# A long convolution and a gated MLP on one core: when tiles are loaded and turned

## The chip, the cores and the metric

The kernel runs on one core of a Trainium2 chip. The metric is device time in microseconds (us), the median of several executions; lower is better. A core has a matrix engine (TensorE, PE in the profile, with its weight loads as PEld), a vector engine (DVE), a scalar engine (ACT), a general one (POOL), and a queue that here issues every transfer (SP). Each works through its own list of instructions in order, and they wait for each other by semaphores.

## The reference

Two blocks follow each other. The first is a long convolution, done in the reference by FFT:

```
h_filt = (maximum(pos_emb @ w1, 0) @ w2) * exp(-0.01 * pos)
u = x * v                                  # (4, 12480, 128)
y = irfft(rfft(u, 2S) * rfft(h_filt, 2S))[:, :S]
x1 = (x * y).reshape(49920, 128)
```

The second is an MLP with 2048 hidden units over the 49920 rows of the first:

```
h = x1 @ w_in                              # (49920, 2048)
out = (h * cos(h)) @ w_out                 # (49920, 128)
```

All is float32.

## The kernel before

**Two streams in one list.** The convolution of each of the four batches is cut into stages of matrix products: u (products and sums on DVE and POOL, no PE work), f1 and f2 (the forward transform and the product with the filter's spectrum), i1 and i2 (the inverse transform). Each stage is a generator of units (`units`): a unit's matmuls go to a PSUM bank called cv, and its results are read out of the bank while the next unit's matmuls run. The filter, the first batch's u, f1, f2 and i1, and the tables come first, up to about 281 us. After that the rest of the convolution is woven into the MLP by a pacer.

**Tiles and chunks.** The MLP takes its rows in 98 tiles: tile 0 has 104 rows of four tokens each, the others 128 (up to 512 tokens). A tile has 16 chunks of 128 hidden units. For chunk i (`moe_up`) PE multiplies the turned tile `at` by a slice of `w_in` into a phase bank ph (line 139); ACT (L871) and DVE (L872) reduce the phase; a chunk later ACT takes the sine (L877) and DVE multiplies (L878, `moe_act`, called by `act`), which frees ph. POOL forms sums (L886, L889, L890), and seven chunks later PE multiplies by `w_out` into acca or accb (L903). The sums of a tile are read out by `moe_evict` (L918 to L924) into `ot`.

**The pacer.** `convolve` adds one step to what is owed at each chunk and runs the generators until nothing is owed. A yield is worth, for instance, 1.0 step for a unit of f1, 3.4 for one of f2, 0.8 for one of i1; i2 of the first batch takes 3.5 steps a unit, that of the next two 3.4, of the last 1.5. A unit of i2 makes 104 rows of z, which DVE forms from the bank (L585) and SP stores to memory (`zd`, L589). `made` counts these units. A stage's rest yields 3.0, scaled in i2.

**Loading and turning.** `load(n)` has SP bring the rows of tile n into one of three `at` buffers (L846). If the rows are not made yet, it first runs the convolution until they are, without counting it as owed. The rows are turned by four PE transposes of 128x128 into a cv bank (L143, `moe_turn`), which ACT copies back over the rows (L859, `moe_turned`). In the other direction a finished tile is turned back by four transposes into a phase bank (`moe_back`, L143 too), copied by ACT (L938, `moe_rows`) and stored (L949, `moe_store`).

**The batch of transposes.** Before the change, in each odd tile n, SP is given the loads of n + 1 and n + 2 at chunk 2 (`SOON`), and at chunk 10 (`AT`) all transposes come together: `act` of chunk 9 and the convolution step of chunk 10 are issued early, then `turns(n)` puts tile n + 1 into a cv bank, tiles n - 2 and n - 1 out into two phase banks, and tile n + 2 into the same cv bank as n + 1 (into a second one once the convolution is over). The output stores follow at chunk 12.

**Banks.** Eight PSUM banks: two for acca and accb, three for ph, and for cv two while the first batch's i2 runs (a table has the third) and three afterwards. A bank is handed out again in the order in which its last reader was issued.

**Order on SP.** Loads for the convolution go ahead of their unit: `tm` (tables of i2) and `xs` one unit ahead (two in the last batch), `h` and `w` for f2 two units ahead, `xt` and `vt` for u one ahead. A load waits on SP until its buffer is free, and all that stands behind it waits too.

Of the kernel before, what the change touches and what calls it, by code (L numbers as in the profile page):

```python
# [34 lines left out]
def kernel(  # L35
# [68 lines left out]
    NFC = DFF // P  # L104
# [4 lines left out]
    NALL = 1 + math.ceil((NROWS - R) / P)  # L109
# [2 lines left out]
    ALONE = 8  # L112
    XV = 36
    LATER = 96
    SOON = 2
    AT = NFC // 2 + 2
    WCOL = 256

# [22 lines left out]
    def transpose(dst, src, ident):  # L141
        n = src.shape[0]
        nc.tensor.transpose(dst, src, ident[0:n, 0:n])  # L143
# [231 lines left out]
    def filter_turn(pool, bank, pe, ident):  # L375
        pt = bank()
        for q in range(ROWS // 2):
            transpose(pt[:, q * 2 * H:(q + 1) * 2 * H], pe[:, q, :], ident)
        peT = pool.tile([P, ROWS * H], F32, name="peT", bufs=3)
        nc.scalar.copy(out=peT[:, :], in_=pt[:, 0:ROWS * H])  # L380
        return peT
# [138 lines left out]
    soon = slice(0, CB // 8), slice(CB // 8, CB)  # L520
# [316 lines left out]
    def first_row(n):  # L837
        return min(R + (n - 1) * P, NROWS) if n else 0

    def rows_of(n):  # L840
        return first_row(n + 1) - first_row(n)

    def moe_load(pool, n):
        m, row = rows_of(n), first_row(n)
        zb = pool.tile([P, G, D], F32, name="at", bufs=3)
        nc.sync.dma_start(zb[0:m, :, :], zd[row:row + m, :, :])  # L846
        zbs[n] = zb

    def moe_turn(n, pt):
        m = rows_of(n)  # L850
        for i in range(G):
            transpose(pt[:, i * m:(i + 1) * m], zbs[n][0:m, i, :], ident)

    def moe_turned(pool, n, pt):

        m, zb = rows_of(n), zbs.pop(n)
        at = zb if n else pool.tile([P, G, D], F32, name="at", bufs=3)
        ats[n] = at[:, :, :].rearrange("p g d -> p (g d)")
        nc.scalar.copy(out=ats[n][:, 0:G * m], in_=pt[:, 0:G * m])  # L859

    def phase_bank(c):
        late = made[0] == B * NG and c % 2
        return bank() if late else ps_h.tile([P, BANK], F32, name="ph")
# [12 lines left out]
    def moe_act(ph, part, scale):  # L876
        nc.scalar.activation(part, part, AF.Sin, scale=scale)  # L877
        nc.vector.tensor_tensor(part, ph, part, op=ALU.mult)  # L878
# [14 lines left out]
    def moe_down(n, pair, second, b11, b21, b22, t):  # L893

        r = rows_of(n)
        if pair == 0:
            sums[n, second] = ps_acc.tile([P, 4, P], F32, name="acc" + "ab"[second])
        acc = sums[n, second]
        todo = ((3, 6, b22), (0, 1, t[1]), (1, 4, t[0]), (2, 3, t[3])) if second else \
            ((0, 0, b11), (2, 2, b21), (1, 5, t[2]))  # L900
        for i, (place, weight, right) in enumerate(todo):
            for h in range(2):
                nc.tensor.matmul(acc[h * CB:(h + 1) * CB, place, 0:r],  # L903
                                 w_out_sb[:, pair, weight, :], right[:, h * r:(h + 1) * r],
                                 start=(pair == 0 and i == 0), stop=(pair == NFC // 2 - 1),
                                 skip_group_check=True)

    def moe_evict(pool, n, second, ot=None):
        r = rows_of(n)
        acc = sums.pop((n, second))  # L910

        def twice(a):
            return bass.AP(tensor=a.tensor, offset=a.offset, ap=[a.ap[0], [0, 2], a.ap[1]])

        if not second:
            ot = pool.tile([P, 4, P], F32, name="ot", bufs=2)
            nc.scalar.copy(out=ot[:, 2, 0:r], in_=acc[:, 0, 0:r])
            nc.vector.tensor_tensor(ot[:, 0:2, 0:r], acc[:, 1:3, 0:r], twice(ot[:, 2, 0:r]),  # L918
                                    op=ALU.add)
            return ot  # L920
        nc.vector.tensor_tensor(ot[:, 2:4, 0:r], acc[:, 0:2, 0:r], twice(ot[:, 0, 0:r]),
                                op=ALU.add)
        nc.vector.tensor_tensor(ot[:, 0, 0:r], acc[:, 1, 0:r], ot[:, 2, 0:r], op=ALU.add)
        nc.vector.tensor_tensor(ot[:, 2:4, 0:r], acc[:, 2:4, 0:r], ot[:, 2:4, 0:r], op=ALU.add)  # L924
        return ot

    def moe_back(n, ot):
        m = rows_of(n)
        pt = ps_h.tile([P, BANK], F32, name="ph")
        places = pt[:, :].rearrange("p (h i e d) -> p h e i d", h=2, e=2, d=CB)  # L930
        for i, block in enumerate((1, 2, 3, 0)):
            transpose(places[0:m, i // 2, i % 2], ot[:, block, 0:m], ident)
        return pt

    def moe_rows(n, ot, pt):

        m = rows_of(n)
        nc.scalar.copy(out=ot[0:m, :, :].rearrange("p g d -> p (g d)"), in_=pt[0:m, :])  # L938
        return ot
# [15 lines left out]
    with tc.manual_schedule():  # L955
        with tc.tile_pool(name="psum", bufs=8, space=PSUM) as psum, \
                ExitStack() as first:
            def bank():
                return psum.tile([P, BANK], F32, name="ps")
# [142 lines left out]
        ps_c = [two_banks]  # L1102
        mpool = ctx.enter_context(tc.tile_pool(name="moe", bufs=2))

        def bank():
            return ps_c[0].tile([P, BANK], F32, name="cv")


# [15 lines left out]
        def load(n):  # L1124
            while made[0] * R < first_row(n + 1):
                next(conv)
            moe_load(mpool, n)
# [3 lines left out]
        pt = bank()  # L1131
        moe_turn(0, pt)
        moe_turned(mpool, 0, pt)
        steps = [(n, c) for n in range(NALL) for c in range(NFC)]
        hidden, pairs, gates, ots, obs = {}, {}, {}, {}, {}

        def convolve():
            nonlocal owed
            owed += 1.0
            while owed > 0.0:  # L1140
                owed -= next(conv, owed)

        def act(i):
            if i in hidden:
                moe_act(*hidden.pop(i))

        def turns(n):

            ins = [k for k in (n + 1, n + 2) if k < NALL]
            outs = [(k, ots.pop(k)) for k in (n - 2, n - 1) if k in ots]  # L1150
            alone = made[0] == B * NG
            banks = [bank() for k in ins[0:1]]
            for k in ins[0:1]:
                moe_turn(k, banks[0])
                moe_turned(mpool, k, banks[0])
            copies = []
            for k, ot in outs:
                copies.append((k, ot, moe_back(k, ot)))
            for k in ins[1:2]:
                if alone:  # L1160
                    banks.append(bank())
                moe_turn(k, banks[-1])
            yield
            for k, ot, pt in copies:
                obs[k] = moe_rows(k, ot, pt)
                yield
            for k in ins[1:2]:
                moe_turned(mpool, k, banks[-1])

        for i in range(len(steps) + LAG):  # L1170
            if i >= LAG:
                pn, pc = steps[i - LAG]
                moe_down(pn, pc // 2, pc % 2, *gates[i - LAG - pc % 2])
                if pc >= NFC - 2:
                    ots[pn] = moe_evict(mpool, pn, pc % 2, ots.get(pn))
            rest = iter(())
            if i < len(steps):
                n, c = steps[i]
                both = n % 2 == 1 and c == AT
                if n == 0 and c == NFC // 2:  # L1180
                    load(1)
                if n % 2 == 1 and c == SOON:
                    for k in range(n + 1, min(n + 3, NALL)):
                        load(k)
                if n == 0 and c == NFC - 2:
                    pt = bank()
                    moe_turn(1, pt)
                    moe_turned(mpool, 1, pt)
                if both:
                    act(i - 1)  # L1190
                    convolve()
                    rest = turns(n)
                    next(rest)
                ph = phase_bank(c)
                next(rest, None)
                if c % 2 == 0:
                    pairs[i] = mpool.tile([P, 2, BANK], F32, name="gt", bufs=4)
                hidden[i] = moe_up(mpool, n, c, pairs[i - c % 2], ph)
            for _ in rest:
                pass  # L1200
            act(i - 1)
            if i - 4 in pairs:
                gates[i - 4] = moe_sums(mpool, steps[i - 4][0], pairs.pop(i - 4))
            if i < len(steps) and c == AT + 2:
                for k in sorted(obs):
                    moe_store(k, obs.pop(k))
            if i >= len(steps) or not both:
                convolve()
        for n in sorted(ots):
            moe_store(n, moe_rows(n, ots[n], moe_back(n, ots[n])))  # L1210
# [28 lines left out]
```

## Time and profile before

| | us |
|---|---|
| median of 3 runs (3618.9 to 3620.81) | 3619.49 |
| the profiled execution | 3619.85 |
| its span, first to last instruction | 3618.1 |

Stages of that execution, from windows cut at the first matmul of a chunk:

| window, us | what runs | length | PE busy | DVE | ACT | POOL |
|---|---|---|---|---|---|---|
| 0 to 281.4 | filter, first batch's forward transform, tables | 281.4 | 266.7 | 227.1 | 199.7 | 206.0 |
| 281.4 to 530.9 | tiles 0 to 6, first batch's i2, second batch's u | 249.5 | 238.6 | 208.0 | 163.8 | 216.5 |
| 530.9 to 1082.8 | tiles 7 to 22, second batch's f1, f2, i1 | 551.9 | 546.6 | 428.7 | 337.1 | 423.9 |
| 1082.8 to 1122.1 | chunk 1 of tile 23: a run of convolution alone | 39.3 | 36.5 | 30.3 | 14.0 | 3.2 |
| 1122.1 to 1961.2 | tiles 23 to 46 | 839.1 | 831.4 | 652.5 | 493.2 | 652.2 |
| 1961.2 to 1979.6 | the same kind of run in tile 47 | 18.4 | 15.5 | 11.7 | 5.0 | 3.5 |
| 1979.6 to 2816.0 | tiles 47 to 70 | 836.4 | 831.1 | 651.9 | 493.5 | 652.2 |
| 2816.0 to 2830.8 | the same kind of run in tile 71 | 14.8 | 13.6 | 11.4 | 5.1 | 3.5 |
| 2830.8 to 2960.5 | tiles 71 to 73, last batch's i2 | 129.7 | 129.7 | 79.7 | 55.8 | 60.2 |
| 2960.5 to 3618.1 | tiles 74 to 97, MLP alone | 657.6 | 650.2 | 519.8 | 452.3 | 525.9 |

A view of waits names who waited, on which tile and line, for whom, with the total, the count and the longest. The timeline merges equal instructions: start, length, engine, line, operation, tiles, shape, count, and in brackets the idle time before it with what ended it. Matmuls are pipelined, so a busy PE can still be slowed; the granted clock (1.00 is full) is a column of the windows.

### The profile page before, as it was taken

The numbers are of one execution on the slowest core, as the hardware profiler recorded it, in microseconds if no ns is written. First come the engines' busy times: TensorE is split into PE (matmuls) and PEld (weight loads), VectorE is DVE, ScalarE is ACT, GpSimd is POOL, SyncE is SP. The second block draws the span as 40 slices with busy tenths as digits, with TensorE's granted clock in tenths as the row PEclk, the third lists the DMA queues.
The fourth block names the chain that finished last, engine by engine and source line by source line (L and its number), as shares of the span: only waits on it lengthen the run. The fifth ranks groups of instructions, "written<-read, shape, count | busy, mean of one in ns | idle before, by whom it ended". The sixth has DMA issues, their size and how long they took to land.

```text
span 3618.1 us, 102337 instructions
## 1 busy us (share of the span) xinstructions
PE 3559.8 (98%) x40830; PEld 2553.9 (71%) x40830; DVE 2821.0 (78%) x5289; ACT 2219.4 (61%) x4482; POOL 2747.0 (76%) x3240
## 2 busy tenths in 40 slices
PE   9999999999999999999999999999999999999999
PEld 7996767666677777666677776766667876666666
DVE  7887886688887775688887776678887667877877
ACT  7776666656654556656554556666655446666676
POOL 7777995688864996688864887579884457878887
PEclk9999999999999999999999999999999999999999
DMA  7545540122214640022211662022220440000000
GB/s 192 157 147 158 154 125 14 37 66 71 76 32 115 172 139 27 24 72 75 66 36 48 171 175 62 13 61 66 73 71 20 133 123 25 16 22 25 16 22 17
DMA packets 224196, 281.86 MB, mean 78 GB/s; under 512 B 23386, under 2 KB 161122, under 8 KB 223594
## 3 DMA queue, kind: packets, MB, share of 16 engines
q1 hardware_dynamic: 223722, 275.30, 26.5%
q8 instruction: 326, 5.34, 0.6%
q14 instruction: 148, 1.21, 0.1%
HBM read 194.75 MB, written 80.46 MB: 76 GB/s over the span
## 4 chain that ended last, share of the span: by engine, by line
PE 86%; DVE 3%; ACT 1%; POOL 1%; DMA 1%; issue 1%; SPq 0%; ACTq 0%; DVEq 0%; POOLq 0%
PE ph L139 31%; PE accb L903 18%; PE cv L139 17%; PE acca L903 13%; PE cv L457 3%; PE cv L143 1%; PE ph L143 1%; DVE gt L872 1%; DVE gt L878 1%; ACT gt L871 0%; DMA tm<-td 0%; DVE xt L439 0%; POOL ts L886 0%; DVE t L516 0%; POOL slots L449 0%
## 5 line engine op out<-in xcount | busy, mean ns | idle before, releaser
L871 ACT ACTIVATE gt<-ph 128x512 int32<-128x512 f32 (+1 forms) x1374 | 818.9, 596 | 1165.3 <-PE ph L139 1083.5
L872 DVE SCALAR_TENSOR_TENSOR gt<-ph,gt 128x512 f32<-128x512 f32 (+1 forms) x1374 | 943.4, 687 | 681.5 <-ACT gt L871 676.7
L139 PE MATMUL ph<-at,w_in_sb 128*64 128x512 f32 (+1 forms) x5496 | 1428.5, 594 | 6.1 <-DVE gt L878 4.7
L886 POOL TENSOR_TENSOR ts<-gt 128x512 f32<-128x512 f32 (+2 forms) x784 | 1000.9, 1277 | 537.0 <-PE accb L903 525.4
L877 ACT ACTIVATE gt<-gt 128x512 f32<-128x512 f32 (+1 forms) x1568 | 973.3, 621 | 14.8 <-DVE gt L872 13.6
L878 DVE TENSOR_TENSOR gt<-ph,gt 128x512 f32<-128x512 f32 (+1 forms) x1374 | 930.9, 678 | 1.4
L903 PE MATMUL accb<-ts,w_out_sb 128*64 128x128 f32 (+2 forms) x9408 | 652.9, 272 | 0.0
L889 POOL TENSOR_TENSOR ts<-ts,gt 128x256 f32<-128x256 f32 (+2 forms) x784 | 574.0, 732 | 61.5
L890 POOL TENSOR_TENSOR ts<-gt,ts 128x256 f32<-128x256 f32 (+2 forms) x784 | 573.4, 731 | 61.5
L903 PEld LDWEIGHTS acca<-gt,w_out_sb 128*64 128x64 f32 x6272 | 403.1, 136 | 245.6 <-issue 209.5
L903 PEld LDWEIGHTS accb<-ts,w_out_sb 128*64 128x64 f32 x9408 | 546.7, 137 | 0.0
L903 PE MATMUL acca<-gt,w_out_sb 128*64 128x128 f32 (+2 forms) x6272 | 482.1, 272 | 0.0
L903 PEld LDWEIGHTS accb<-gt,w_out_sb 128*64 128x64 f32 x3136 | 228.4, 136 | 246.0 <-issue 186.4
L139 PEld LDWEIGHTS ph<-at,w_in_sb 128*64 128x64 f32 x5496 | 353.2, 137 | 28.4 <-issue 13.1
L139 PEld LDWEIGHTS cv<-slots,tm 96*40 96x40 f32 (+1 forms) x3840 | 228.6, 126 | 127.8 <-issue 118.4
L903 PE MATMUL accb<-gt,w_out_sb 128*64 128x128 f32 (+1 forms) x3136 | 314.0, 273 | 2.4 <-DVE ot L924 0.4
L903 PE MATMUL acca<-ts,w_out_sb 128*64 128x128 f32 (+1 forms) x3136 | 311.6, 272 | 2.3 <-POOL ts L889 2.3
L139 PE MATMUL cv<-slots,tm 96*40 96x128 f32 (+1 forms) x3840 | 256.0, 275 | 9.9 <-DMA tm<-td 5.5
L517 POOL TENSOR_TENSOR slots<-slots,t 120x256 f32<-120x256 f32 x288 | 210.9, 734 | 67.8 <-DVE t L516 60.8
L139 PEld LDWEIGHTS cv<-even,slots 120*33 120x33 f32 (+1 forms) x3072 | 166.7, 125 | 65.0 <-issue 58.8
L903 PEld LDWEIGHTS acca<-ts,w_out_sb 128*64 128x64 f32 x3136 | 204.5, 137 | 3.7 <-POOL ts L889 3.6
L139 PE MATMUL cv<-at,w_in_sb 128*64 128x512 f32 (+1 forms) x776 | 200.5, 587 | 0.0
(142 smaller groups left out, 3822.5 us busy)
## 6 DMA issues: line engine op xcount, KB each, us to landing
h<-hd SPq DMA_DIRECT2D x144, 240.0 KB
tm<-td SPq DMA_DIRECT2D x96, 312.0 KB
xt<-in_x_dram SPq DMA_DIRECT2D x120, 208.0 KB
xs<-in_x_dram SPq DMA_DIRECT2D x120, 208.0 KB
zd<-xs SPq DMA_DIRECT2D x119, 208.0 KB
at<-zd SPq DMA_DIRECT2D x96, 256.0 KB
vt<-in_v_dram SPq DMA_DIRECT2D x90, 208.0 KB
w<-wd SPq DMA_DIRECT2D x144, 105.0 KB
```

The costliest lines, as they stand in the source:

```text
L139: nc.tensor.matmul(dst[lo:hi], left[:, lo:hi], right, start=start, stop=stop)
L143: nc.tensor.transpose(dst, src, ident[0:n, 0:n])
L457: nc.tensor.matmul(dst[lo:hi], u[:, b, lo:hi, i], c1[0:u.shape[0], r:r + 2, :].rearrange("p r k -> p (r k)"), start=True, stop=True)
L517: nc.gpsimd.tensor_tensor(y[:, r], y[:, r], t[:, r], op=op)
L871: nc.scalar.activation(turns, ph[:, 0:m], AF.Identity, bias=phase)
L872: nc.vector.scalar_tensor_tensor(out=part, in0=ph[:, 0:m], scalar=phase, in1=turns, op0=ALU.add, op1=ALU.subtract)
L877: nc.scalar.activation(part, part, AF.Sin, scale=scale)
L878: nc.vector.tensor_tensor(part, ph, part, op=ALU.mult)
L886: nc.gpsimd.tensor_tensor(ts[:, 0:2, 0:half], gt[:, :, half:2 * half], gt[:, 0, 0:2 * half].rearrange("p (h n) -> p h n", h=2), op=ALU.sub ...
L889: nc.gpsimd.tensor_tensor(t[2], t[1], b11, op=ALU.add)
L890: nc.gpsimd.tensor_tensor(t[3], b21, t[2], op=ALU.subtract)
L903: nc.tensor.matmul(acc[h * CB:(h + 1) * CB, place, 0:r], w_out_sb[:, pair, weight, :], right[:, h * r:(h + 1) * r], start=(pair == 0 and i ...
```

## The change

Four things change in the order of the work; the arithmetic, the shapes and the number of instructions of each kind stay.

1. Tiles 1 to 6 each have a small batch at chunk 10: tile n - 1 out, then tile n + 1 in, with a bank for each. The early `act` is left out there. From tile 7 on odd tiles have the double batch as before.
2. From tile 7 on, if a cv bank was taken in the convolution step of the chunk at hand, and not in both chunks before it, the batch moves on by a chunk, to chunk 13 at the latest. The convolution step and, from tile 7 on, `act` stay early in each chunk from 10 up to the batch.
3. The load of tile n + 2 is at chunk 14 of tile n for n up to 5 and for even n (chunk 15 of tile 0), and at chunk 5 (`SOON`) for odd n from 7 on.
4. The output stores come two chunks after the batch, wherever that is.

```diff
-    SOON = 2
+    SINGLE, SOON = 7, 5
...
         def bank():
+            count[0] += 1
             return ps_c[0].tile([P, BANK], F32, name="cv")
...
+        due, turned, taken = False, -3, {}
         def convolve():
             nonlocal owed
             owed += 1.0
+            before = count[0]
             while owed > 0.0:
                 owed -= next(conv, owed)
+            taken[i] = count[0] - before
+
+        def just_taken(i):
+
+            return taken[i] and not (taken[i - 1] and taken[i - 2])
...
-            ins = [k for k in (n + 1, n + 2) if k < NALL]
+            ins = [k for k in range(n + 1, n + (2 if n < SINGLE else 3)) if k < NALL]
             outs = [(k, ots.pop(k)) for k in (n - 2, n - 1) if k in ots]
             alone = made[0] == B * NG
+            if len(ins) == len(outs) == 1:
+                (k, ot), = outs
+                back = moe_back(k, ot)
+                pt = bank()
+                moe_turn(ins[0], pt)
+                moe_turned(mpool, ins[0], pt)
+                yield
+                obs[k] = moe_rows(k, ot, back)
+                return
...
-                both = n % 2 == 1 and c == AT
+                if c == 0:
+                    due = 0 < n < SINGLE or n % 2
                 if n == 0 and c == NFC // 2:
                     load(1)
-                if n % 2 == 1 and c == SOON:
-                    for k in range(n + 1, min(n + 3, NALL)):
-                        load(k)
+                soon = n + 2 <= SINGLE or n % 2 == 0
+                if soon and c == (NFC - 2 if n else NFC - 1) and n + 2 < NALL:
+                    load(n + 2)
+                if n >= SINGLE and n % 2 and c == SOON and n + 2 < NALL:
+                    load(n + 2)
...
-                if both:
-                    act(i - 1)
+                early = due and c >= AT
+                if early:
+                    if n >= SINGLE:
+                        act(i - 1)
                     convolve()
-                    rest = turns(n)
-                    next(rest)
+                    if n < SINGLE or c == AT + 3 or not just_taken(i):
+                        due, turned = False, i
+                        rest = turns(n)
+                        next(rest)
...
-            if i < len(steps) and c == AT + 2:
+            if i == turned + 2:
                 for k in sorted(obs):
                     moe_store(k, obs.pop(k))
-            if i >= len(steps) or not both:
+            if not early:
                 convolve()
```

More of the change, by code (lines that the diff above doesn't have):

```diff
@@ L1103 @@
         mpool = ctx.enter_context(tc.tile_pool(name="moe", bufs=2))
+        count = [0]
         def bank():
+            count[0] += 1
             return ps_c[0].tile([P, BANK], F32, name="cv")
@@ L1175 @@
                     ots[pn] = moe_evict(mpool, pn, pc % 2, ots.get(pn))
-            rest = iter(())
+            rest, early = iter(()), False
             if i < len(steps):
                 n, c = steps[i]
-                both = n % 2 == 1 and c == AT
+                if c == 0:
+                    due = 0 < n < SINGLE or n % 2
                 if n == 0 and c == NFC // 2:
                     load(1)
-                if n % 2 == 1 and c == SOON:
-                    for k in range(n + 1, min(n + 3, NALL)):
-                        load(k)
+                soon = n + 2 <= SINGLE or n % 2 == 0
[3 more added lines that the diff above has]
+                    load(n + 2)
                 if n == 0 and c == NFC - 2:
```

## The prediction

> **What bounds the kernel.** I read the page's first part and its chain first, then the waits of TensorE (PE), then the stages by windows, then the timeline around each wait.
>
> ```profile
> span 3618.1 us, 102337 instructions
> PE 3559.8 (98%) x40830; PEld 2553.9 (71%) x40830; DVE 2821.0 (78%) x5289; ACT 2219.4 (61%) x4482; POOL 2747.0 (76%) x3240
> PE 86%; DVE 3%; ACT 1%; POOL 1%; DMA 1%; issue 1%; SPq 0%; ACTq 0%; DVEq 0%; POOLq 0%
> ```
>
> PE is busy 98% and carries the chain: only 58 us of the span are not PE's. The change adds and removes no matmul, so it can only move PE's waits and what hangs on them. These are the waits it can reach (PE's waits: us in total, times, longest):
>
> ```profile
> PE cv L139 <- DMA tm<-td: 5.5, 4, 1.8
> PE cv L143 <- DVE t L516: 5.5, 5, 1.5
> PE cv L143 <- issue: 4.4, 3, 2.8
> PE cv L143 <- DVE xs L585: 3.7, 2, 2.3
> PE cv L143 <- ACT at L859: 2.5, 1, 2.5
> PE cv L143 <- DMA at<-zd: 1.4, 2, 0.9
> ```
>
> L143 into cv is a tile's transposition, L139 into cv from tm the inverse transform's last stage. Windows show a second cost (length, busy time of PE, PEld, DVE, ACT, POOL, granted clock, DMA share, GB/s):
>
> ```profile
> 336.99:340.40 3.41, 3.16 (x12) 1.60 (x14) 0.00 (x0) 0.71 (x3) 3.33 (x5) 0.50 0.49 138
> 412.08:415.49 3.41, 3.41 (x16) 3.09 (x16) 0.15 (x1) 1.17 (x2) 3.25 (x5) 0.50 0.63 189
> 483.77:487.18 3.41, 1.90 (x34) 1.64 (x30) 3.31 (x7) 2.74 (x6) 2.72 (x4) 1.00 0.43 134
> 1118.65:1122.06 3.41, 1.71 (x32) 1.50 (x29) 0.69 (x1) 0.00 (x0) 0.00 (x0) 1.00 0.71 219
> 1122.06:1125.47 3.41, 3.41 (x24) 2.19 (x22) 0.71 (x2) 1.11 (x2) 0.00 (x0) 0.50 0.49 130
> 351.80:386.40 34.60, 34.34 (x436) 25.22 (x434) 30.77 (x56) 23.52 (x51) 33.35 (x41) 1.00 0.53 151
> ```
>
> After the waits at 334.7, 409.2, 1119.5 and 1976.6 us the clock is halved for 3.41 us. The starts of these stretches lie whole multiples of 3.413 us apart. A grid cell in which PE idled 1.70 us was enough, one with 1.51 us (483.77) was not. The last line is tile 2, the yardstick of a tile without transposes.
>
> [...]
>
> **Part A, single transposes up to tile 6.** Now tiles 1, 3 and 5 take 39.3, 41.6 and 39.8 us between the starts of their first matmuls; tiles 2 and 4 take 34.6 and 34.5. The three batches so cost 17.1. Sixteen transposes (four of each of four tiles) take 1.92 from 957.25 to 959.17 where nothing waits, 0.12 each; the three batches hold 44, or 5.4. So 11.7 is waiting and half clock. The number of transposes stays (44 + 16 with tile 7's; then 48 + 12), as does every DMA.
> Tile 1 loses its 2.54: the second tile's transposes no longer share the bank that ACT must copy (at 336.62, queued behind L877 and two table steps). Next late is chunk 10's phase bank, freed by L878 of chunk 8 (334.87 + 0.67 = 335.54); PE is ready near 334.7: 0.85 stays. In tile 3 PE waits from 409.21 to 411.99 for L585 (411.21 + 0.68), behind two L878 (409.79, 1.51 long). One of them now comes later, minus 0.7, and the outgoing transposes (0.5) go first: 1.5 stays. Tile 5, 2.27, likewise: 1.1. For tiles 2, 4 and 6 the trace has no batch; between 0 and the 1.5 of tile 3 I take 0.5 each. Three more entries into transposes: 0.3 each (PEld's "issue" gap before a change of shape, 0.28 to 0.29). In a single batch ACT's two copies (0.57 and 0.59) stand ahead of L877 of the chunk before and L878 is late behind them; the bank that needs it is asked for two chunks on, some 4 us, which hides it (else 1.2 a batch, rival 1). New: 0.85 + 1.5 + 1.1 + 1.5 + 0.9 = 5.85. **A = 11.7 - 5.85, a gain of 5.8** (bounds 0 and 11).
>
> **Part B, a chunk later behind a new bank.** I counted the pacing by the code: each chunk owes one step, a unit of f2 is 3.4 steps. The count puts a unit's bank into the very step of the batch at tiles 13, 17, 35, 41 and 65 of the f2 stretches, the five that wait for t L516. In the new count 13, 17, 35 (and 39, 59) move to chunk 11, while 41 and 65 have the bank one chunk earlier, as tiles 19 and 61 have now, without a wait. **Gain 5.5.** In the i2 stretches tiles 23, 27, 47, 51 and 71 move too, in i1 tile 21. Chunk 10 then does its convolution step before its own matmul, and L877/L878 of chunk 9 run early, as in every batch now. SP is passed by no further instruction except the output stores, two chunks behind the batch as before.
>
> **Part C, the loads.** An even tile's load moves from chunk 2 to chunk 14 of the tile before (4 earlier), the odd one's from 2 to 5. On SP each so passes about one unit's loads (tm, xs or h, w) and one zd store; its buffer was freed with the last chunk of the tile before last, so it holds up nothing there except where its rows are just being stored, right behind a run. A load whose rows aren't made runs the convolution until they are, without MoE work. The count: now 36.1 + 3.4 steps at tile 23, 14.9 + 3.4 at 47, 12.5 at 71; then 40.1 at tile 22, 18.5 at 46, 8.8 at 71. Steps cost the same in a run and outside, so I cost them at nothing: a 0.8-step unit of i1 takes 0.82 us in the run (DVE's two L563, 0.40 each), 1.02 a step; tile 22, paced with i1, takes 42.6 us against 26.2 of a tile after the last convolution, 1.02 a step too. The second forced pair vanishes, and with it this (timeline of PE):
>
> ```profile
> 1115.60 3.85 PE L139 MATMUL cv<-slots,tm 96*64 96x128 f32 x64 [0.94 <-DVE slots L563]
> 1121.15 1.18 PE L139 MATMUL cv<-slots,tm 96*64 96x128 f32 x16 [1.70 <-DMA tm<-td]
> 1122.11 1.93 PE L139 MATMUL ph<-at,w_in_sb 128*64 128x512 f32 x4
> 1123.81 1.86 PE L139 MATMUL cv<-slots,tm 96*64 96x128 f32 x16
> 1126.16 1.03 PE L139 MATMUL ph<-at,w_in_sb 128*64 128x512 f32 x4
> 1128.38 1.10 PE L139 MATMUL cv<-slots,tm 96*64 96x128 f32 x16 [1.20 <-DMA tm<-td]
> ```
>
> The third unit of i2 follows in the same run, before its tm (issued 1117.73) is there. In the new order chunk 14's and 15's work lies between: some 4 us of PE against the missing 1.70. Waits 1.70 + 1.20, and 1.80 in the third batch; half clock 0.90 + 0.76 here (1.93 against 1.03, 1.86 against 1.10), 0.90 + 0.36 there. **Gain 7.6** (bounds 0, if tm is late again, and 7.6). The 0.94 stays.
> The waits for at (0.94 and 0.50, tiles 29 and 53): SP sends those loads at 1348.36, held by a vt load until 1348.00; the even one now stands before that vt load. **Gain 1.4.** The odd one still goes at 1348.4 and has until the thirteenth transpose, 1353.5.
>
> **Against it**: tile 45's batch (0.57 now) gets two banks in its step, and the moved batches in i1 and i2 have no row; nearest is 0.48 at tile 27. I set 2 us (0 to 6).
>
> **Sum.** 5.8 + 5.5 + 7.6 + 1.4 - 2 = 18.3. The profiled execution took 3619.85 us (span 3618.1), 0.36 over the median 3619.49: 3619.49 - 18.3 = 3601, **I say 3602.**
>
> **Rivals.**
> 1. Singles gain nothing. For: in tile 2 POOL is busy 33.35 of 34.60 and DVE 30.77, so six batches may each leave a backlog. Against: PE still does 34.34. A = 0: 3602 + 5.8 = 3608. Chance 0.12.
> 2. The wait for tm stays, because SP is held by the at load in front of it (SP sent at at 1122.16 and the next tm only at 1122.61). C's 7.6 goes: 3609.5. Against: the tm of the third unit stands before the at load. Chance 0.10.
> 3. The waits that stay trip the clock. They fall elsewhere on the grid: tile 3's 1.5, tile 5's 1.1, and the 2.34 at 533.86 (DVE/POOL sums before the second batch's first stage), which misses it now. At 1.3 to 1.7 each: 3602 + 4.5 = 3606.5. [...] Chance 0.08.
> 4. The moved batches only move their wait: B = 0 and 0.5 for each of eleven: 3602 + 5.5 + 5.5 = 3613. Against: tiles 19 and 61 have that very distance and no wait. Chance 0.07.
> 5. Slower: the odd tile's rows come too late. In f2 SP stands behind each unit's h load (it waited 503.8 us in 101 times for t L516), so a load of chunk 5 goes out at chunk 5.3 to 7.8, and lands 3.8 us on (1348.36 to the transposes at 1352.16), by chunk 9.8 of about 1.9 us each. If one more unit comes between, the fifteen f2 batches wait 1.9 each: 3602 + 28.5 = 3630. From 1.2 us a batch on the change loses. Against: the second set starts only 1.4 us after the first. Chance 0.06.
> The forecast itself: 0.57, its own range 3597 to 3608.
>
> **Numbers.** A change under 0.2% (7.2 us) can hardly be told from none here. Faster by more: forecast and rivals 1 to 3, 0.87, less 0.07 where two of them meet: 0.80. Same: 0.07 + 0.07 = 0.14. Slower 0.06. The range reaches from A's upper bound (3596) to just short of rival 4: 3595 to 3612.
>
> **What would show it.** Right: no "DVE t L516" and no "ACT at L859" among PE's waits; clock 0.50 after 1100 us gone; tiles 1 to 6 about 212 us instead of 218.4; the run of convolutions at tile 22, chunk 14. Wrong: waits of L143 on at in f2 (rival 5), tm waits behind the runs (2), new half-clock stretches (3).

## The result and the profile after

| | us |
|---|---|
| before, median of 7 runs (3614.92 to 3624.68) | 3619.49 |
| changed, median of 7 runs (3603.94 to 3609.85) | 3608.43 |
| ratio, with its 95% interval | 0.9966 (0.9954 to 0.9978) |
| profiled execution of the changed kernel (span) | 3609.03 (3607.2) |

The change gains 11.1 us where 17.5 were forecast: faster, inside the range, and 6.4 us short. The page of the changed kernel, its span, engines and chain:

```profile
span 3607.2 us, 102415 instructions
PE 3558.6 (99%) x40830; PEld 2547.6 (71%) x40830; DVE 2833.6 (79%) x5289; ACT 2223.3 (62%) x4482; POOL 2745.2 (76%) x3240
PE 88%; DVE 3%; ACT 1%; issue 1%; POOL 1%; DMA 0%; ACTq 0%; DVEq 0%; POOLq 0%
```

PE's busy time is the old one less 1.2 us; what went is idle time, as the change adds and removes no matmul. PE's waits now (us in total, times, longest):

```profile
PE ph L139 <- DVE gt L878: 5.4, 12, 1.0
PE cv L143 <- ACT at L859: 4.5, 8, 0.7
PE accb L903 <- DVE ot L924: 2.6, 4, 1.1
PE cv L457 <- POOL slots L449: 2.4, 1, 2.4
PE cv L143 <- issue: 1.6, 2, 1.1
...
PE cv L143 <- DVE xs L585: 1.4, 1, 1.4
...
PE cv L143 <- ACT other L561: 1.1, 1, 1.1
```

Gone are "DMA tm<-td" (5.5), "DVE t L516" (5.5) and "DMA at<-zd" (1.4), all three as predicted. But "ACT at L859" has grown from one wait of 2.5 to eight of at most 0.7, "accb <- DVE ot L924" from 0.4 to 2.6, and "ACT other L561" is new. The forced run now ends in ordinary work (PE's timeline in tile 22):

```profile
1108.83 2.97 PE L139 MATMUL cv<-slots,tm 96*64 96x128 f32 x48 [0.94 <-DVE slots L563]
...
1112.49 1.06 PE L139 MATMUL cv<-slots,tm 96*40 96x128 f32 x16
```

The 0.94 at its head stays, as foretold; the unit of 16 matmuls behind it takes 1.06, not the 1.86 of half clock, and nothing waits for tm.

Cutting the traces at the first matmul of each tile shows where the 10.9 us between the two spans lie. The other columns belong to experiments below; "again" is a second profile of the changed kernel, and "best" is the last kernel of the experiments (planned, tile 39 by two chunks, load at chunk 2).

| stage | before | changed | again | loads alone | all at chunk 10 | planned | best |
|---|---|---|---|---|---|---|---|
| before tile 0 | 281.4 | 283.3 | 282.1 | 282.2 | 283.4 | 283.2 | 282.4 |
| tile 0 | 31.0 | 31.9 | 29.6 | 29.6 | 31.9 | 31.8 | 29.6 |
| tiles 1 to 6 | 218.4 | 213.3 | 213.6 | 217.3 | 213.2 | 213.2 | 213.2 |
| tile 7 | 41.2 | 42.5 | 40.8 | 41.2 | 42.5 | 42.5 | 42.1 |
| tile 13 | 33.8 | 33.5 | 33.5 | 33.8 | 33.8 | 32.7 | 32.7 |
| tile 17 | 33.9 | 33.7 | 33.6 | 33.9 | 33.8 | 33.2 | 33.2 |
| tile 21 | 36.5 | 37.7 | 37.8 | 36.5 | 36.5 | 36.4 | 36.5 |
| tiles 22 to 25 | 190.7 | 186.8 | 186.7 | 186.7 | 186.7 | 186.8 | 186.7 |
| tiles 26, 27 | 71.7 | 71.9 | 72.0 | 71.2 | 71.3 | 71.2 | 71.1 |
| tiles 34 to 43 | 317.8 | 316.6 | 316.5 | 317.2 | 317.3 | 316.6 | 314.9 |
| tiles 46 to 49 | 167.8 | 164.5 | 164.6 | 165.3 | 164.5 | 164.5 | 164.4 |
| tiles 50, 51 | 71.7 | 71.8 | 71.8 | 71.2 | 71.2 | 71.2 | 71.1 |
| tiles 58 to 67 | 317.5 | 316.1 | 316.3 | 316.4 | 316.8 | 316.0 | 316.1 |
| tiles 68, 69 | 82.5 | 83.6 | 83.6 | 83.6 | 83.8 | 83.8 | 83.8 |

Tiles 8 to 12 and 74 to 97 are alike in before and changed, within 0.1.

### The profile page after: what moved, and what is told of

The parts are those of the page before. It is cut to its first block, busy times and chain, and to the rows that moved or that the text cites. A ratio compares the mean times of both kernels' runs of the same rounds, so it can differ in the third digit from the quotient of the medians.

```text
span 3607.2 us, 102415 instructions
## 1 busy us (share of the span) xinstructions
PE 3558.6 (99%) x40830; PEld 2547.6 (71%) x40830; DVE 2833.6 (79%) x5289; ACT 2223.3 (62%) x4482; POOL 2745.2 (76%) x3240
## 3 DMA queue, kind: packets, MB, share of 16 engines
q1 hardware_dynamic: 223722, 275.30, 27.1%
## 4 chain that ended last, share of the span: by engine, by line
PE 88%; DVE 3%; ACT 1%; issue 1%; POOL 1%; DMA 0%; ACTq 0%; DVEq 0%; POOLq 0%
PE ph L139 32%; PE accb L903 18%; PE cv L139 18%; PE acca L903 14%; PE cv L457 3%; PE cv L143 1%; PE ph L143 1%; DVE gt L878 1%; DVE gt L872 1%; ACT gt L871 0%; DVE xt L439 0%; POOL ts L886 0%; ACT at L859 0%; POOL slots L449 0%; DVE slots L563 0%
## 5 line engine op out<-in xcount | busy, mean ns | idle before, releaser
L872 DVE SCALAR_TENSOR_TENSOR gt<-ph,gt 128x512 f32<-128x512 f32 (+1 forms) x1376 | 944.8, 687 | 650.4 <-ACT gt L871 645.5
L139 PE MATMUL ph<-at,w_in_sb 128*64 128x512 f32 (+2 forms) x5504 | 1427.9, 594 | 6.8 <-DVE gt L878 5.4
L877 ACT ACTIVATE gt<-gt 128x512 f32<-128x512 f32 (+1 forms) x1568 | 973.3, 621 | 26.8 <-DVE gt L872 25.6
L878 DVE TENSOR_TENSOR gt<-ph,gt 128x512 f32<-128x512 f32 (+1 forms) x1376 | 932.5, 678 | 10.6 <-ACT gt L877 9.1
L903 PEld LDWEIGHTS acca<-gt,w_out_sb 128*64 128x64 f32 x6272 | 401.0, 136 | 250.8 <-issue 213.2
L139 PEld LDWEIGHTS cv<-even,slots 120*64 120x64 f32 (+1 forms) x3072 | 166.1, 125 | 62.2 <-issue 55.3
```

The source lines that it names most:

```text
L139: nc.tensor.matmul(dst[lo:hi], left[:, lo:hi], right, start=start, stop=stop)
L872: nc.vector.scalar_tensor_tensor(out=part, in0=ph[:, 0:m], scalar=phase, in1=turns, op0=ALU.add, op1=ALU.subtract)
L903: nc.tensor.matmul(acc[h * CB:(h + 1) * CB, place, 0:r], w_out_sb[:, pair, weight, :], right[:, h * r:(h + 1) * r], start=(pair == 0 and i ...
```

## The experiments

Ratios are to the kernel before on the same chip, with 95% intervals. Its medians on the three chips are 3619.09 (beside single transposes, delay and loads alone, and the copy ahead of the early `act`), 3619.51 (beside the kernels with two chunks for tile 39 and the changed kernel again) and 3620.16 (beside the other four). Each diff is against the kernel before where it says so, else against the changed one.

**Single transposes alone** (against before):

```diff
-    SOON = 2
+    SINGLE, SOON = 7, 2
...
-                both = n % 2 == 1 and c == AT
+                both = (0 < n < SINGLE or n % 2 == 1) and c == AT
...
-                    act(i - 1)
+                    if n >= SINGLE:
+                        act(i - 1)
```

with the single path in `turns` as in the change.

> Only the single batches of tiles 1 to 6, on the kernel before (loads and double batches as before). Part theory: the three parts are independent, so tiles 1 to 6 are as short as in the changed kernel (213.3 us instead of 218.4), and nothing else moves but tile 7: in all 4 to 6 us faster than before, about 3614. Rival (the singles are only good with the earlier loads, since the second tile's rows are then there): tiles 2, 4 and 6 wait for at and the gain is under 2 us.

3616.49 (3610.83 to 3618.91): 0.9988 (0.998 to 0.9997). In the profile tiles 1 to 6 take 213.4 instead of 218.4. The medians differ by 2.6, less than the 4 to 6 expected; the interval, 1.1 to 7.2 us of gain, holds the predicted 5.8. The profiled execution is the shortest of the twelve (mean clock 0.999), with no half clock in it except at the very end, so that profile alone would overstate the gain.

**The delay alone:**

```diff
-    SINGLE, SOON = 7, 5
+    SINGLE, SOON = 0, 2
...
-                    if n < SINGLE or c == AT + 3 or not just_taken(i):
+                    if n < 7 or c == AT + 3 or not just_taken(i):
```

with the loads as before and without the single path.

> Only the batch that moves a chunk behind a new bank, on the kernel before. Moved-wait theory: the waits for t L516 go (5.5 us before), and each moved double batch gets a wait of 0.5 to 0.7 for ACT's copy L859; batches at tiles 13, 17, 35, 41, 65 move, and in i1 and i2 some more: 1 to 3 us faster than before, about 3617. Rival (the delay is worth the whole 5.5, and the changed kernel lost it to its other loads): about 3614, no waits for L859.

3618.4 (3615.88 to 3623.95): 0.9997 (0.9989 to 1.0006). No gain can be told. The waits for t L516 are gone, and eight waits for at L859, 6.2 us in all, stand in the list (2.6 of them is tile 1's old one).

**The loads alone** (against before; from tile 8 on):

```diff
-                if n % 2 == 1 and c == SOON:
-                    for k in range(n + 1, min(n + 3, NALL)):
-                        load(k)
+                if n % 2 == 1 and n < SINGLE and c == 2:
+                    for k in range(n + 1, min(n + 3, SINGLE + 1)):
+                        load(k)
+                if n >= SINGLE - 1 and n % 2 == 0 and c == NFC - 2 and n + 2 < NALL:
+                    load(n + 2)
+                if n >= SINGLE and n % 2 and c == SOON and n + 2 < NALL:
+                    load(n + 2)
```

> Only the loads of tiles 8 and up moved, batches as before. Part theory: the forced second unit of i2 goes, with the waits for tm and the half-clock stretches at about 1122 and 1979 us: tiles 22 and 23 together 4 to 5 us shorter, tiles 46 and 47 together 3 to 4.2; about 3611. Rival (the waits for tm went only because the batch came later): they stay here, and the time is within 2 us of before.

3609.03 (3606.88 to 3617.38): 0.9973 (0.9965 to 0.9982), 10.1 us: by the medians nearly the whole gain. But seven of its twelve executions have a mean clock of 0.999, and only two of the seven of the changed kernel. At the same mean clock the changed kernel is shorter, on average 3604.0 against 3608.2 at 0.999 and 3608.9 against 3611.8 at 0.998. In the profile tiles 22 and 23 fall by 4.9 and tiles 46 and 47 by 4.2, as expected. Its waits of PE:

```profile
PE cv L143 <- DVE t L516: 5.5, 5, 1.5
...
PE cv L139 <- DMA tm<-td: 0.6, 1, 0.6
```

The first line is the old one to the digit, so this kernel still has all that the delay was to remove; the second had 5.5 before. Although L516's total is unchanged, it isn't the same five tiles: the earlier runs shift the count of banks, so that 41 and 65 no longer have theirs in the batch's step and 39 and 59 do. Tiles 34 to 43 and 58 to 67 gain 0.6 and 1.2 here without any delay.

**No delay, the rest as changed:**

```diff
-                    if n < SINGLE or c == AT + 3 or not just_taken(i):
+                    if True:
```

> The changed kernel with all batches at chunk 10 (singles and loads as changed). If the delay is worth what its profile shows, 1.6 us in the f2 stretches against 1.3 lost in tile 21, this is within 1 us of the changed kernel: 3608 to 3609, with t L516 back in five batches (5.5 us) and tile 21 at 36.5 us. Rival (the prediction's own term): 5.5 us slower, 3614.

3606.99 (3605.47 to 3608.54): 0.9961 (0.9948 to 0.9973), not distinguishable from the changed kernel (3608.43, and 3606.74 in a second set). Its list of waits has the old line again:

```profile
PE cv L143 <- DVE t L516: 5.5, 5, 1.5
```

So the delay takes away 5.5 us of waits, and no gain in the time can be told; the rival's 3614 is out. The table says where they went: against this column the changed kernel gains 0.3, 0.1, 0.7 and 0.7 in the stages with moved f2 batches, and loses 1.3 in tile 21 and 0.6 in each of the pairs 26, 27 and 50, 51. In tile 21 (PE, changed kernel):

```profile
1025.93 0.63 PE L143 MATMUL cv<-ident,at 128*128 128x128 f32 x4 [1.06 <-ACT other L561]
```

**Where the moved batch waits.** In the changed kernel's tile 13, PE, ACT and DVE around the batch at chunk 11 (timelines of the three):

```profile
766.76 0.66 PE L143 MATMUL cv<-ident,at 128*128 128x128 f32 x4
...
768.92 0.66 PE L143 MATMUL cv<-ident,at 128*128 128x128 f32 x4 [0.63 <-ACT at L859]
```

```profile
767.76 0.64 ACT L877 ACTIVATE gt<-gt 128x512 f32<-128x512 f32 x1 [1.31 <-DVE gt L872]
768.30 0.56 ACT L859 COPY at<-cv 128x512 f32<-128x512 f32 x1
```

```profile
766.39 0.41 DVE L514 TENSOR_TENSOR slots<-cv,h 120x256 f32<-120x256 f32 x1
766.72 0.41 DVE L516 TENSOR_TENSOR t<-cv,h 120x256 f32<-120x256 f32 x1
767.05 0.68 DVE L872 SCALAR_TENSOR_TENSOR gt<-ph,gt 128x512 f32<-128x512 f32 x1
```

Read backwards: the second tile's transposes need the bank that ACT's copy (L859) empties. The copy stands behind L877 of chunk 10, which waits 1.31 for L872 of chunk 10. And L872 stands behind L514 and L516, because chunk 10's convolution step was issued ahead of that chunk's own matmul, although the batch wasn't there any more. Two edits follow from this.

**The copy ahead of the early `act`:**

```diff
             for k in ins[0:1]:
                 moe_turn(k, banks[0])
                 moe_turned(mpool, k, banks[0])
+            act(i - 1)
...
                 if early:
-                    if n >= SINGLE:
-                        act(i - 1)
                     convolve()
```

> The changed kernel, with ACT's copy L859 of the first turned tile ahead of the sine L877 of the chunk before, in the double batches from tile 7 on. Queue theory: the copy is late only because L877 stands before it, which waits for L872, so PE's waits for L859 (4.5 us, 8 times) go and the f2 stretches get 3 us shorter: about 3604. Rival (distance theory: the moved batch has one convolution step less between chunk 10 and itself, so something of that chunk is late in any order): the wait goes on to L878 and the phase banks, and the time stays at 3608.

3614.33 (3609.5 to 3615.84): 0.9982 (0.9974 to 0.9991), worse than the changed kernel. Its waits:

```profile
PE ph L139 <- ACT ot L938: 8.4, 25, 0.4
...
PE ph L143 <- DVE gt L878: 4.1, 8, 0.6
...
PE cv L143 <- ACT at L859: 0.2, 1, 0.2
```

The wait for L859 is all but gone, from 4.5 to 0.2: the copy behind L877 was its cause. But the edit holds for every double batch: 24 of them, 20 never moved, now wait up to 0.35 before the next phase bank, which ACT's copy of the outgoing tile (L938) leaves later (the 25th wait is tile 1's, in the changed kernel too), and six of the moved ones wait 0.5 for L878, which the later `act` holds back (the other two of the eight are in the changed kernel as well). Neither theory expected that price. A moved batch gains by it (tile 13 takes 33.1 instead of 33.5), one that stayed loses (tile 9 takes 38.9 instead of 38.5), and more stayed than moved. So the order inside a batch is not the thing to change; the chunk ahead of it is the other suspect.

**The batch moved without the early order in chunk 10.** Five f2 batches are named; the others stay at chunk 10:

```diff
+    MOVED = (13, 17, 35, 39, 59)
...
-                early = due and c >= AT
+                early = due and c >= AT + (n in MOVED)
...
-                    if n < SINGLE or c == AT + 3 or not just_taken(i):
-                        due, turned = False, i
-                        rest = turns(n)
-                        next(rest)
+                    due, turned = False, i
+                    rest = turns(n)
+                    next(rest)
```

> The changed kernel, but the batch moves a chunk only in the five f2 tiles that have the new bank at chunk 10 (13, 17, 35, 39, 59), chosen ahead, and chunk 10 of these keeps the usual order (its own matmul before its convolution step); i1 and i2 batches stay at chunk 10. Distance theory: the moved batches' wait for L859 comes from chunk 10's matmul standing behind its convolution step; with the usual order the five are as batches at tiles 15 and 19, without t L516 and without L859, some 0.6 us better each, and tile 21 is 1.3 us shorter: 4 us faster than the changed kernel, about 3604. Rival (the wait belongs to the place itself, DVE's reads of the new bank): waits of 0.5 to 0.7 stay at the five tiles, and only tile 21's 1.3 is won: 3607.

3602.71 (3599.97 to 3605.04): 0.9947 (0.9933 to 0.996), 4.3 us below the kernel without any delay beside it. At the same mean clock the gap is 3.5 (0.998) and 4.6 (0.999), on average, and 3.2 of it stand in the four rows of the table with moved f2 batches (tile 13, tile 17, tiles 34 to 43, tiles 58 to 67). Lines are numbered one higher here. Tile 13, PE and then ACT:

```profile
766.48 0.66 PE L144 MATMUL cv<-ident,at 128*128 128x128 f32 x4
...
767.85 0.62 PE L144 MATMUL cv<-ident,at 128*128 128x128 f32 x4
```

```profile
766.45 0.63 ACT L878 ACTIVATE gt<-gt 128x512 f32<-128x512 f32 x1 [0.24 <-DVE gt L873]
767.18 0.59 ACT L860 COPY at<-cv 128x512 f32<-128x512 f32 x1
```

From the first transposes to the second set is 1.37 us, where the changed kernel takes 2.16: the activation (L878 here) starts at 766.45 instead of 767.76 and no longer stops the copy. The edit also puts chunk 10's early `act` back in its usual place. The path read above does not run through it, but no run changes the one without the other.

Four of the five batches wait for nothing. The fifth doesn't follow:

```profile
1685.79 0.66 PE L144 MATMUL cv<-ident,at 128*128 128x128 f32 x4 [1.31 <-DVE t L517]
```

At tile 39 there is no matmul of the convolution between its new bank at chunk 10 and the batch at chunk 11, so one chunk is no distance at all.

**Two chunks for tile 39**, and **the second load at chunk 2 in place of 5**: on the changed kernel, on the planned one, and on the one with two chunks. The edits are

```diff
-    MOVED = (13, 17, 35, 39, 59)
+    MOVED = {13: 1, 17: 1, 35: 1, 39: 2, 59: 1}
...
-                early = due and c >= AT + (n in MOVED)
+                early = due and c >= AT + MOVED.get(n, 0)
```

```diff
-    SINGLE, SOON = 7, 5
+    SINGLE, SOON = 7, 2
```

> The changed kernel with the second tile's rows loaded at chunk 2 again instead of 5 (the first tile's stay at chunk 14 of the tile before). Even-load theory: what took the forced second unit away is the first tile's earlier load alone; by the count the second load forces nothing at chunk 2 either, so tiles 22 and 23 (115.6 us) and 46 and 47 (93.5) stay within 0.5 us, and the time at 3608. Rival (chunk 5 matters, since at chunk 2 the second load holds up SP right behind the run): waits for tm come back, up to 3 us behind each of the two runs, 3612 or more.

> The planned batches of the run before together with the second load at chunk 2. If both parts act by themselves, the sum of the two: 3604. If chunk 5 was needed, 3607 or more.

> The planned batches (five f2 tiles moved, usual order in the chunks before), but tile 39's two chunks on: at chunk 11 no convolution matmul stood between the new bank and the batch, and 1.31 us of t L516 stayed. Distance theory: that wait goes too, 1 us better than with one chunk; 5 us faster than the changed kernel on the same chip, 3603. Rival (the wait follows DVE's reads and not PE's distance): 0.5 us or more stays at tile 39.

> The same with the second load at chunk 2. Its stages differ in the profiles by some tenths only (tiles 70 to 73 0.6 shorter, 48 and 49 0.8 longer), so within 1 us of the kernel before this one: 3603. Rival (the 2.9 us between the earlier pair, with chunk 5 and chunk 2, are the loads' own): 3600.

| | load at 5 | load at 2 |
|---|---|---|
| changed | 3608.43, again 3606.74 | 3605.17, 0.9956 (0.9943 to 0.9968) |
| planned | 3602.71 | 3599.85, 0.9944 (0.9932 to 0.9957) |
| planned, 39 by two | 3603.29, 0.9951 (0.9938 to 0.9965) | 3599.93, 0.9943 (0.993 to 0.9955) |

Two chunks at tile 39 take its last wait for L516 away and tiles 34 to 43 from 316.6 to 314.9, but no gain shows in the medians: 3603.29 is 3.5 below the changed kernel beside it, where 5 were expected. With the load at chunk 2 the median is some 3 us lower in each row (against the first set of the changed kernel; 1.6 against the second), and the tm waits behind the runs don't come back: the gain of the loads is in the even tile's earlier load, and the later odd one brings nothing here.

None of the three expectations for the load at 2 had this: 3608, 3604 and 3603 were expected, and only the rival of the last named 3600. Of the 3 us the profiles explain 0.5 to 0.6 (tiles 70 to 73). Much of the rest is the clock that an execution drew: three of the fifteen with the load at 2 have a mean clock of 0.998, twelve of the twenty-two with the load at 5. At the same clock the planned kernels lie closer: at 0.998 3604.9 and 3605.0 with the load at 5 against 3603.5, at 0.999 3600.0 and 3602.7 against 3599.8 and 3603.3. Whether the load at 2 makes the higher clock likelier no run settles.

A short wait ahead of a unit of i2 in tile 48 comes and goes between these kernels (0.6 with the loads alone and with planned and load at 2, 1.3 with 39 by two and load at 5, none in the other profiles of the table), and no run settles what sets it.

**The changed kernel again**, on the chip of the last two:

> The changed kernel once more, beside the two that follow: 3608, with 3604 in the executions whose mean clock is 0.999 and 3608 to 3610 in those with 0.998, as in its first seven.

3606.74 (3604.29 to 3608.75): 0.996 (0.9948 to 0.9973). The last kernel of the table, 3599.93 (3597.84 to 3602.52) beside it, is 6.8 us faster, and the two sets of runs don't overlap: it beats both kernels. Of the expectation, the two shortest executions (3604.3 and 3604.4, mean clock 1.000 and 0.999) and the longest (3608.8, at 0.998) fit; the other two, 3606.7 at 0.999 and 3607.1 at 0.998, lie between. This second profile also prices chance. It is 4.6 us shorter than the first (spans 3602.6 and 3607.2), and the table shows where: 1.2 before tile 0, 2.3 in tile 0 and 1.7 in tile 7; all else together is 0.5 longer. Windows on the clock's grid around the first f1 unit of tile 7, in the first profile and then in the second (length, busy time of PE, PEld, DVE, ACT, POOL, granted clock, DMA share, GB/s):

```profile
531.30:534.71 3.41, 1.05 (x11) 0.70 (x13) 1.64 (x3) 1.02 (x2) 3.33 (x5) 1.00 0.00 0
534.71:538.12 3.41, 3.41 (x23) 2.81 (x21) 0.00 (x0) 0.00 (x0) 3.25 (x4) 0.50 0.61 152
```

```profile
525.67:529.08 3.41, 2.26 (x20) 1.01 (x16) 2.81 (x5) 2.23 (x4) 3.33 (x6) 1.00 0.03 7
529.08:532.49 3.41, 2.05 (x23) 1.70 (x25) 0.81 (x2) 0.00 (x1) 3.25 (x5) 1.00 0.12 34
```

It is the same wait of 2.4 us for POOL's L449. In the first profile it falls into one cell of the grid, 2.36 idle, and the next cell runs at half clock. In the second it is shared by two cells, 1.15 and 1.36, and nothing happens.

## Why the prediction was right in direction and short in size

**Part A, "a gain of 5.8": right, somewhat too large.** Tiles 1 to 6 fall by 5.1. But with the loads or the delay alone, whose batches there are the old ones, they take 217.3 and 217.1: their profiles have one half-clock stretch where the kernel before has two (3.41 each, from 336.99 and 412.08). So 1.1 to 1.3 of the 5.1 are the clock in one execution, and 3.8 to 4.0 are the batches; that includes the stretch behind tile 3's wait of 2.78, which all three profiles with the old batches show and none of the ten with single ones. Of the single waits, tile 1 keeps 1.00 (0.85 foretold), tile 3 has 0.62 (1.5) and tile 5 has 0.89 (1.1). Rival 1, that singles gain nothing, didn't occur.

**Part B, "Gain 5.5": the step that failed.** The argument was the distance: "41 and 65 have the bank one chunk earlier, as tiles 19 and 61 have now, without a wait". That part held, for there is no wait for t L516 left. What it priced at nothing is the order in the chunk that the batch leaves. It saw that "Chunk 10 then does its convolution step before its own matmul" and passed over it with "as in every batch now"; but in every batch now the transposes follow in that same chunk. In a moved batch they come a chunk later, where ACT's copy stands behind L877 of chunk 10, and so behind the L872 that the early convolution step holds back. Tiles 19 and 61 are no precedent, since their batch is in the first early chunk. Seven of the eleven moved batches wait 0.51 to 0.73 for the copy (4.2 together) and tile 21 waits 1.06 for L561: 5.3, about as much as the 5.5 that went. So the prediction's own sign of being right, no "ACT at L859" among PE's waits, failed. This is rival 4 in half: the wait did move, by its 0.5 each, but the old one didn't stay as well, so it cost the gain and no more. The planned order shows the cause for the f2 batches: with chunk 10 in its usual order the waits for the copy vanish, four of the five batches wait for nothing at all, and 4.3 us come. For the batches in i1 and i2 no run changes the order alone; there the planned kernel only leaves them at chunk 10.

**Part C, "Gain 7.6": right.** Tiles 22 to 25 and 46 to 49 fall by 3.8 and 3.3, 7.1 together: the three waits for tm and the half-clock stretches at 1122 and 1979 are gone, net of about 1 us given back in each place, in the two tiles behind the run. Rival 2 (tm waits stay) and rival 5 (odd rows late) didn't occur.

**The waits for at, "Gain 1.4": too large.** The waits went, and tiles 28, 29 and 52, 53 are 1.6 shorter. But 1.0 of the 1.2 at tiles 52, 53 also came in the two kernels that keep the old loads: the kernel before had a fourth wait for tm there, 0.83 at 2161.85, which neither of them has and which the prediction left out of its sum. So no more than about 0.5 is due to the loads. Near the old places there are new waits, 1.10 and 1.13 for the sums (L924, at 1342.41 and 2193.51), and 0.57 for L878 at each batch: in the first, DVE gets to the sums late, behind an L439 of 1.13.

**The margin, "I set 2 us": used up, elsewhere.** Tile 21's 1.3 belongs in part B's account above. Tiles 68, 69 take 1.0 more, with the loads alone as well, but that is work and not a wait: PE has 1136 matmuls there instead of 1120, and the 16 are the convolution's.

**Rival 3, waits trip the clock: true of some executions.** It named the 2.34 us wait at 533.86, and that one does it in this profile (2.36 idle in one cell, the next at a granted 0.50): 1.7 us in tile 7 against the second profile. A second stretch, two cells from 282.1 on, costs 2.3 in tile 0; no rival named it, though the kernel before has one of a single cell at 282.38 that the prediction's list of stretches leaves out. The change doesn't make the wait of tile 7, which is in the kernel before too. Whether it makes the stretch likelier the profiles don't settle: five of thirteen show one there, all five among the nine whose kernels have both single batches and earlier loads. The two shortest of the seven runs of the changed kernel (3603.9 and 3604.1) have a mean clock of 0.999, the other five (3608.4 to 3609.9) 0.998.

In sum, for the two profiles, of which the forecast's 18.3 came to 10.9: B's 5.5 is the largest term that fell away (its batches give back what they gain), A and the waits for at were too large by 1 to 2 and by 1, and 4.1 were lost before tile 0, in tile 0 and in tile 7, for which the sum has no term. Gains at tiles 34 to 43 and 58 to 67, which come with the loads alone and which it didn't forecast, make up for part. The 4.1 are chance: in the second profile of the same kernel these three stages are 1.1 shorter than in the kernel before, and its span is 15.5 below. So the median gain of 11.1 depends on luck as well: with more executions at the higher clock it would have come nearer to the forecast, for a reason that is not in the forecast's sum.

## What to carry to other kernels

When a step is moved one slot later, what was issued early for its sake must move with it: here the convolution step stayed early in the slot that the batch had left, and the new wait ate the whole gain. Ask of a moved step not only how far it now stands from its producer, but what stands ahead of its consumers on their engine (here L877 ahead of the copy L859 on ACT: 4.5 us of waits, 0.2 with the copy first). And where half clock follows a wait in one execution and not in the next, as at tile 7 here (granted clock 0.50 and 1.00), profile one program twice before putting a few microseconds down to an edit, and compare executions of equal mean clock.

## What the runs showed of the hardware

The half-clock stretches (granted clock 0.50) start at whole multiples of 3.413 us from each other in every profile that has more than one: in the kernel before 16, 38, 246, 497 and 976 such cells behind the first, at 282.38, in the changed one 74 and 973 behind the first, at 282.13. The grid lies differently in each execution (cells start at 531.30 in the first profile of the changed kernel and at 525.67 in the second, 1.65 cells earlier). A stretch lasts one such cell (in three profiles two, 6.83, at tile 0, as from 282.13 in the changed kernel); only the one at the end of every profile is longer, 4.20 to 6.96. At the wait of tile 7, cells with 2.03 to 2.50 us of idle PE were followed by half clock (five profiles; 2.36 in the changed kernel) and cells with up to 1.95 weren't (eight; 1.37 at most in the kernel before). Elsewhere the limit isn't as clean: in the changed kernel the cell from 278.72, with 1.41 idle, was followed by it, and the one ahead, from 275.30, with 1.53, wasn't. Nor was the 1.51 at 483.77 of the kernel before, or one with 1.70 at 1113.5 (single transposes alone), while the 1.70 at 1118.6 and the 1.80 at 1975.4 of the kernel before were. So the prediction's "1.70 us was enough" is no threshold; idle time by itself doesn't decide, and what does wasn't found. Counting the transposes (L143) as idle doesn't decide either: in the kernel before the cell from 893.36 has 0.89 idle and 1.99 of transposes, and the next runs at full clock (1.00).

Which clock an execution draws shows in its time: the kernel before took 3614.6 to 3618.3 us at a mean clock of 0.999 and 3623.7 to 3626.9 at 0.996.
